# Seven-product feed-forward kernel: the planner's transfer times, SP costs and conversion dates changed

## The chip, the cores and the metric

The kernel runs on one core of a Trainium2 chip. The metric is the device time of one execution in microseconds (us), here always on that one core. Five engines work side by side, each through its own list of instructions in order: TensorE (PE, the matmuls; PEld is its weight load), VectorE (DVE), ScalarE (ACT), GpSimd (POOL, unused here after the start) and SyncE (SP), which issues nearly all DMA transfers. An engine whose next instruction waits for something executes nothing behind it meanwhile.

## What is computed

A channel attention over 6016 tokens of 256 channels feeds two feed-forward layers with 2048 hidden columns:

```python
qn = q / (norm(q, axis=1) + 1e-6);  kn = k / (norm(k, axis=1) + 1e-6)
s = kn.transpose(0, 2, 1) @ qn / tau            # 256 x 256
a = exp(s - s.max(-1));  a /= a.sum(-1) + 1e-9
x = v @ a
x = square(maximum(x @ w_in1, 0)) @ w_out1      # layer 1
out = leaky(x @ w_in2, 0.01) @ w_out2           # layer 2
```

The weights of both layers arrive as 64-bit floats and are turned into 32-bit ones on the chip.

## The kernel before

**Tiling.** The tokens are cut into six passes of two halves, each half 512 tokens wide (448 in the fifth pass): `WIDTH`, `NP` = 6. The hidden columns are cut into eight groups of 256, `NG` = 8. A unit is one group of one pass of one layer, 96 in all, numbered n. Every operand is split into a high and a low part (`round` or `cast` on ACT makes the high part, `low` on DVE the rest), and a product is three matmuls. From the second pass on, the first product of a unit is computed in seven block products instead of eight (F1 to F7, `product`), with sums of blocks of x and of weights prepared beforehand; ACT copies and DVE additions (`c11`, `c22`, `c21`, `c12`, lines 564 and 566) put the results together as c. The second products (`second`, `shared`) add into the banks y.

**Stages.** The attention takes the first 50 us. Layer 1 has a first pass, in which the weights of layer 1 are converted (`convert`) and folded with the attention (`fold`), and five more; layer 2 has six. During a pass of layer 1 the x of the next pass is prepared (`prepare_x`): two halves of v are loaded (`load_v`, line 236, each as four DMAs), DVE transposes them into the single buffer `xr` (line 245), ACT and DVE split them into the x tiles (line 1148 and `low`, line 116) and DVE forms differences (lines 1154 and 1157). The outputs of a pass of layer 1 leave the y banks at the start of the next pass (`take_out`, line 747, into a buffer o; `put` stores it in two DMAs), and layer 2 reads them back (`load` in `prepare_x`, line 1131). The weights of layer 2 are converted in sixteen units during layer 1: `u.load` (line 144) brings 512 KB into one of three buffers `wst`, DVE and ACT work on them, `u.round` writes the buffer `wis` (one only) for eleven of the sixteen, and `u.store` (lines 213 and 215) puts the result into DRAM. `load_wi` (lines 1185 and 1213) and `load_wo` (line 1227 and following) bring them back for every unit.

**The order.** Nothing is ordered by hand. `build` makes a list of tasks: engine, cost, due time, dependences, and the buffers taken and used. `link` sorts each kind of buffer by due time; a buffer's taker waits for the users of the one as many places back as there are buffers, and starts after the taker just before it in the line. `simulate` is a list scheduler: each engine that is free takes, among its tasks that are ready, the one with the earliest due time. A task that depends on another is ready `lat` after that one's end. The starts found are the order in which the instructions are emitted. Only this order reaches the chip: the engines there wait on semaphores, not on planned times. `build` runs three times, each with the starting times (`base[n]`) of the one before. The unit of time is one 512-column matmul. DVE and ACT steps cost what they take (3 for an addition of 512 columns, 5.4 for a `low` of 1024). Every SP task costs 1, however many DMAs it issues, and its data is taken as landed `LOAD` = 22 later (the read-back of x: 55).

**Due times that matter here.** With t0 the start of a pass, the v halves of the next pass are due at t0 + 46 and t0 + 76, the o buffers at t0 + 44 and t0 + 74; both are of the kind `v`, of which there are three. The transposes are due from t0 + 100 on. The conversions of layer 2 are due evenly between the start of the third pass (`base[2 * NG]`) + 60 and the start of layer 2 (`base[6 * NG]`) - 60; their weight loads are due 72 units ahead of that and become ready when the first pass has ended (`begin`) and a `wst` buffer is free.

```python
b.alloc.deps += line[k - b.bufs].users          # link
x = min((x for x in open_[e] if x.ready <= t), key=lambda x: x.due)   # simulate
```

Of the kernel before, what the change touches and what calls it, by code (L numbers as in the profile page):

```python
# [31 lines left out]
def attn_moe_moe2(  # L32
# [715 lines left out]


    tasks, lines = [], {}  # L750

    class Buf:

# [5 lines left out]
    class Task:  # L759


        def __init__(self, engine, cost, due, fn, *args, deps=(), alloc=None, uses=(), lat=0.3):
            self.engine, self.cost, self.due, self.fn, self.args = engine, cost, due, fn, args
            self.deps = [x for x in deps if x is not None]
            self.order, self.lat, self.start = [], lat, None
            self.item = None
            if alloc is not None:
                alloc.alloc = self
                alloc.users.append(self)
            for b in uses:  # L770
                b.users.append(self)
            tasks.append(self)
# [12 lines left out]
    def simulate(pe):  # L785
        for x in tasks:
            x.then, x.then_order = [], []
        for x in tasks:
            x.left, x.ready = len(x.deps) + len(x.order), 0
            for d in x.deps:  # L790
                d.then.append(x)
            for d in x.order:
                d.then_order.append(x)
        free = {"DVE": 13, "ACT": 6, "POOL": 0, "SP": 0, "PE": 0}
        open_ = {e: [] for e in free}
        for x in tasks:
            if not x.left:
                open_[x.engine].append(x)
        n = len(tasks)
        while n:  # L800
            best = None
            for e in ("DVE", "ACT", "POOL", "SP"):
                if open_[e]:
                    t = max(free[e], min(x.ready for x in open_[e]))
                    if best is None or t < best[0]:
                        best = t, e
            t = pe.when(free["PE"])
            if t is not None and (best is None or t < best[0]):
                best = t, "PE"
            if best is None:  # L810
                raise RuntimeError(["stuck"] + [(x.fn.__name__, x.args, [(d.fn.__name__, d.args) for d in x.deps + x.order if d.start is None][:3]) for x in tasks if x.start is None][:12])
            t, e = best
            if e == "PE":
                x = pe.choose(t)
            else:
                x = min((x for x in open_[e] if x.ready <= t), key=lambda x: x.due)
                open_[e].remove(x)
            x.start, x.end = t, t + x.cost
            free[e] = x.end
            n -= 1  # L820
            for d in x.then + x.then_order:
                d.left -= 1
                if x in d.order:
                    d.ready = max(d.ready, t)
                if x in d.deps:
                    d.ready = max(d.ready, x.end + (0 if d.engine == e and x.lat < 1 else x.lat))
                if not d.left and d.engine != "PE":
                    open_[d.engine].append(d)
        return free

    KEEP = 4
    LOAD = 22
    GAPS = {"F2": 1, "F3": 1, "F4": 2}

    class PE:
# [72 lines left out]
    def build(base):  # L908
# [10 lines left out]
        def T(*a, **k):  # L919
            return Task(*a, **k)  # L920
# [18 lines left out]
        def convert(u, due, loaded=None, first=None, pace=4, begin=0):  # L939
            L, g = u.L, u.g  # L940
            d = lambda i: due + i * pace
            blocks = u.blocks
            if loaded is None:
                w = Buf("wst", 3, d(-12))
                t = T("SP", 1, d(-12), u.load, alloc=w, lat=LOAD, deps=[begin] if begin else ())
                deps = [t]
            else:
                w, deps = loaded, ()
            if u is first_o:
                ce = ce_b[0]  # L950
                t = None
            else:
                ce = Buf("ce", 2, d(0))
                t = T("DVE", 1.9, d(0), u.exponent, deps=deps, alloc=ce, uses=[w])
            re = T("ACT", 2.7, d(0.5), u.rebias, deps=[t], uses=[ce])
            cm = Buf("cm", 2, d(1))
            t = T("DVE", 1.9, d(1), u.mantissa, deps=deps, alloc=cm, uses=[w])
            ml = T("DVE", 3, d(2), u.mantissa_low, deps=[t], uses=[w, cm])
            t = T("DVE", 3, d(3), u.sign, deps=[re, ml], uses=[w, ce])
            if blocks:  # L960
                raw_ = Buf("whl", 2, d(4))
                t = T("DVE", 3, d(4), u.high, deps=[t], alloc=raw_, uses=[ce, cm])
                for i in range(4):
                    t = T("DVE", 1.1, d(4.2 + i / 10), lambda i=i: (sums if u.kind == "i" else out_sums)(u.x)[i](),
                          deps=[t], uses=[raw_])
                to = Buf("wis", 1, d(5))
                t = T("ACT", 4.6, d(5), u.round, deps=[t], alloc=to, uses=[raw_])
                t = T("DVE", 5.2, d(6), u.low, deps=[t], uses=[raw_, to])
            else:
                t = T("DVE", 3, d(4), u.high, deps=[t], uses=[ce, cm])  # L970
                if (u.kind, L) == ("o", 1):
                    to = wo_b[1, 0, g] = Buf("wo", 4, d(5))
                elif u.kind == "i":
                    to = whl_b[g] = Buf("whl", 2, d(5))
                else:
                    to = Buf("whl", 2, d(5))
                t = T("ACT", 2.7, d(5), u.round, deps=[t], alloc=to, uses=[cm])
                t = T("DVE", 3, d(6), u.low, deps=[t], uses=[cm, to])
            if u.kind == "o" or L == 2:
                stores[u.kind, L, g] = T("SP", 1, d(7), u.store, deps=[t], uses=[to], lat=LOAD)  # L980
            return t

        whl_done = {0: None, 1: None}
# [15 lines left out]
        for n in range(NG):  # L999
# [3 lines left out]
            if g + 1 < NG:  # L1003
# [7 lines left out]
                lo = [T("DVE", 2.5, at0(m["fold_low"] + 2.6 * i), lambda i=i, pw=pw: fold_low(i, *pw[i]), deps=[hi[i]], uses=[b])  # L1011
                      for i in range(KC)]
                pw_after = lo
                stores["i", 1, g + 1] = T("SP", 1, at0(m["fold_low"] + 6), store_folded, g + 1, deps=lo, uses=[b], lat=LOAD)
                wi_ready[1, 0, g + 1] = lo[-1]
            wi = wi_b[1, 0, g]
            cs = [Buf("c", 3, at0(m["relu"][0 if half == 0 else 2])) for half in range(2)]
# [47 lines left out]
        def finish_plain(L, p):  # L1065
# [4 lines left out]
            for half in range(2):  # L1070
# [8 lines left out]
                else:  # L1079
                    a = T("ACT", 2.7 * s, due, take_out, key, 0, deps=done[L, p, half, 0], alloc=o)  # L1080
                b = T("DVE", 3.1 * s, due + 0.1, take_out, key, 1, deps=done[L, p, half, 1] + [a], uses=[o])
                stores["y", L, p, half] = T("SP", 1, due + 3, put, key, deps=[a, b], uses=[o], lat=LOAD)
                if (L, p) == (1, NP - 1) or p < NP - 1:
                    q = (L, p + 1) if p < NP - 1 else (2, 0)
                    for d, t in enumerate((a, b)):
# [7 lines left out]
        def prepare_x(L, p):  # L1093
# [17 lines left out]
            if L == 1:  # L1111
                vs = []
                for half in range(2):
                    v_b[p, half] = Buf("v", 3, t0 + (46, 76)[half])
                    vs.append(T("SP", 1, t0 + (46, 76)[half], load_v, p, half, alloc=v_b[p, half], lat=LOAD))
                for j, (kc, half) in enumerate(((0, 0), (1, 0), (0, 1), (1, 1))):
                    i = SLOT[kc, half]

# [9 lines left out]
            else:  # L1128
# [1 line left out]
                    new()  # L1130
                    nc.sync.dma_start(raw_x(0, 4), x2_d[p][:, :, :w])

                t = T("SP", 1, t0 + 30, load, alloc=xr, lat=2.5 * LOAD, deps=[stores["y", 1, p, 0], stores["y", 1, p, 1]])
                ready.update(dict.fromkeys(range(4), t))

            def split_x(which, i, j, after):
# [40 lines left out]
        def load_wi(n):  # L1177
            L, p, g = units[n]
            b = wi_b[n] = Buf("wi", 3, base[n - 2] + 0.5)
            if n < 2 * NG:  # L1180
# [18 lines left out]
                    nc.sync.dma_start(wi_d[L, g][:, :, 4:], raw(r["w"][:, :, 4:]))  # L1199

                e = base[n] - 12
                t = T("SP", 1, base[n - 2] + 0.5, load, alloc=b, lat=LOAD, deps=[stores.get(("i", 1, g))])
                xb = Buf("whl", 2, e - 25)
                t = T("DVE", 3, e - 25, join, deps=[t], alloc=xb, uses=[b])
                for i in range(4):
                    t = T("DVE", 1.1, e - 20 + i, lambda i=i: r["s"][i](), deps=[t], uses=[xb])
                t = T("ACT", 2.7, e - 10, high, deps=[t], uses=[xb, b])
                wi_ready[n] = T("DVE", 3, e - 5, lows, deps=[t], uses=[xb, b])
                stores["i", 1, g, "s"] = T("SP", 1, e, store, deps=[wi_ready[n]], uses=[b], lat=LOAD)
                return  # L1210

            def load():
                nc.sync.dma_start(raw(wi_tile(L, p, g)[:, :, 1:]), wi_d[L, g][:, :, 1:])

            dep = stores["i", 1, g, "s"] if L == 1 else stores["i", 2, g]
            wi_ready[n] = T("SP", 1, base[n - 2] + 0.5, load, alloc=b, lat=LOAD, deps=[dep])

        def load_wo(n):
            L, p, g = units[n]
# [2 lines left out]
            if form_of(n) == "P":  # L1222
# [3 lines left out]
                        src = src[:, :, :4].rearrange("p a (k b) m -> p a k b m", k=KC)  # L1226
                    nc.sync.dma_start(raw(wo_tile(L, p, g)), src)

                wo_ready[L, p, g] = T("SP", 1, base[n] + 13, load, alloc=b, lat=LOAD, deps=[dep])
                return  # L1230

            def load():
# [8 lines left out]
                t = late_w[n, "S23"] = cpool.tile([P, 2, 2, P], F32R, tag="ce", name="ws")  # L1241
                nc.sync.dma_start(raw(t), wo_d[L, g][:, :, 6:])

            wo_ready[L, p, g] = T("SP", 1, base[n] + 13, load, alloc=b, lat=LOAD, deps=[dep])
            b = wo_b[n, "S1"] = Buf("ws", 2, base[n] + 20)
            wo_ready[n, "S1"] = T("SP", 1, base[n] + 20, load_s1, alloc=b, lat=LOAD, deps=[dep])
            b = wo_b[n, "S23"] = Buf("ce", 2, base[n] + 60)
            wo_ready[n, "S23"] = T("SP", 1, base[n] + 60, load_s23, alloc=b, lat=LOAD, deps=[dep])


        def unit(n):
# [233 lines left out]
        def combine(p):  # L1485
# [27 lines left out]
            for half, parts in enumerate(((("X", 0, y21), ("P1", 1, y11)), (("V", 0, y22), ("U", 1, y12)))):  # L1513
# [3 lines left out]
                for i, (which, d, dep) in enumerate(parts):  # L1517
# [4 lines left out]

                    k = dict(alloc=o, uses=[B[p, which]]) if i == 0 else dict(uses=[o, B[p, which]])
                    ts_.append(T("DVE", 3.1 * s, t0 + 120 + 30 * half + 15 * i, go, deps=[dep, *ts_], **k))
                T("SP", 1, t0 + 80 + 20 * half, put, key, deps=ts_, uses=[o], lat=LOAD)

        conv = [Unit(kind, 2, g) for g in range(NG) for kind in "io"]
        for sweep in range(2 * NP):
# [65 lines left out]
```

## Time and profile before

| | us |
|---|---|
| median of 3 runs | 1058.67 (1057.12 to 1059.61) |
| the profiled execution | 1054.96 |
| its span, first to last instruction | 1053.2 |
| PE busy | 1027.8 (98%) |
| DVE busy | 766.3 (73%) |
| ACT busy | 753.9 (72%) |
| DMA queue of SP | 209.48 MB, 60.9% of 16 engines |

The profile shows one execution. Rows of a timeline give start, duration, engine, line, operation, out<-in, and in brackets how long the engine had been idle before it and what released it. The granted clock is the share of TensorE's full speed that was allowed in a stretch.

### The profile page before, as it was taken

To read this page: it belongs to the slowest core of one execution; us is meant where nothing else is said; L and a number is where in the kernel's file an instruction comes from. 1 tells how busy PE (TensorE), PEld (TensorE's weight loads), DVE (VectorE), ACT (ScalarE), POOL (GpSimd) and SP (SyncE) were. 2 spreads that over 40 slices of the span, in tenths; PEclk is the share of its full clock that TensorE was granted. 3 is DMA by queue.
4 is the path that set the end of the run, shared out by engine and by line. 5 is a ranking of instruction groups with operands and counts; after the bars stand their busy time and mean duration, and the time that the engine had idled before them with its cause. 6 is when DMAs were issued, how large, how long until landed. Compare 5 with 4: busy or idle time off the path is not lost.

```text
span 1053.2 us, 12842 instructions
## 1 busy us (share of the span) xinstructions
PE 1027.8 (98%) x4723; PEld 868.1 (82%) x4723; DVE 766.3 (73%) x1082; ACT 753.9 (72%) x1140; POOL 0.7 (0%) x6
## 2 busy tenths in 40 slices
PE   9999999998989999799999999999999999999997
PEld 8888887886878788698888888888888888998886
DVE  5999889997888964556546777877877887776433
ACT  6798877886787776468767777677677677675653
POOL 0000000000000000000000000000000000000000
PEclk9999999999999999899999999999999999999999
DMA  9785497589779575556535455555655654644521
GB/s 349 261 220 180 159 288 255 174 313 305 223 275 316 198 248 169 146 191 221 168 125 196 169 185 209 174 181 194 177 188 191 184 184 165 192 180 168 177 76 40
DMA packets 118623, 210.96 MB, mean 200 GB/s; under 512 B 49056, under 2 KB 60320, under 8 KB 116512
## 3 DMA queue, kind: packets, MB, share of 16 engines
q1 hardware_dynamic: 117840, 209.48, 60.9%
q8 instruction: 37, 0.61, 0.3%
q10 hardware_dynamic: 720, 0.66, 0.2%
q14 instruction: 26, 0.21, 0.1%
HBM read 171.05 MB, written 39.06 MB: 199 GB/s over the span
## 4 chain that ended last, share of the span: by engine, by line
PE 87%; DMA 7%; DVE 2%; SPq 1%; ACT 1%; issue 0%; ACTq 0%; DVEq 0%
PE y L557 38%; PE ha L557 16%; PE hb L557 12%; PE hc L557 5%; PE h L713 4%; DMA v<-in_v_dram 4%; PE he L557 4%; PE yA L557 3%; PE sT L399 2%; PE y L597 2%; SPq L236 1%; PE pw L265 1%; DMA qk<-in_k_dram 1%; DMA wi<-wis 1%; PE yF L557 1%; DVE xr L245 1%
## 5 line engine op out<-in xcount | busy, mean ns | idle before, releaser
L557 PE MATMUL y<-g,wo 128*128 128x512 f32 (+1 forms) x1938 | 495.9, 386 | 0.0
L557 PEld LDWEIGHTS y<-g,wo 128*128 128x128 f32 x1938 | 365.5, 189 | 68.4
L116 DVE TENSOR_TENSOR g<-c,g 128x1024 fp32r<-128x1024 f32 (+1 forms) x192 | 229.4, 1199 | 44.5 <-ACT g L683 37.5
L557 PE MATMUL ha<-x,wi 128*128 128x512 f32 (+1 forms) x768 | 214.4, 388 | 16.7 <-ACT w L1270 11.9
L557 PEld LDWEIGHTS ha<-x,wi 128*128 128x128 f32 x768 | 143.9, 189 | 45.4 <-ACT w L1270 13.1
L683 ACT CAST g<-c 128x1024 fp32r<-128x1024 f32 (+1 forms) x162 | 167.4, 1034 | 4.1
L557 PE MATMUL hb<-x,wi 128*128 128x512 f32 (+1 forms) x576 | 160.7, 387 | 0.3 <-DVE c L564 0.3
L557 PEld LDWEIGHTS hb<-x,wi 128*128 128x128 f32 x576 | 108.9, 189 | 21.0 <-DVE c L564 0.7
L700 ACT ACTIVATE c<-c 128x512 f32<-128x512 f32 (+1 forms) x144 | 89.7, 623 | 41.5 <-DVE c L566 41.4
L698 ACT ACTIVATE c<-c 128x512 f32<-128x512 f32 (+1 forms) x160 | 97.6, 619 | 27.0 <-DVE c L564 25.6
L557 PE MATMUL hc<-x,wi 128*128 128x512 f32 (+1 forms) x288 | 80.0, 386 | 0.0
L1270 ACT COPY w<-ha 128x512 f32<-128x512 f32 (+1 forms) x64 | 37.0, 578 | 59.5 <-PE ha L557 59.4
L566 DVE TENSOR_TENSOR c<-w,hb 128x512 f32<-128x512 f32 (+1 forms) x44 | 29.7, 674 | 50.5 <-ACT w L1270 50.0
L557 PEld LDWEIGHTS hc<-x,wi 128*128 128x128 f32 x288 | 53.8, 188 | 10.2 <-ACT c L1270 0.4
L557 PE MATMUL he<-x,wi 128*128 128x512 f32 (+1 forms) x216 | 60.2, 387 | 1.0 <-DVE c L564 1.0
L566 DVE TENSOR_TENSOR c<-u,hb 128x512 f32<-128x512 f32 (+1 forms) x44 | 29.7, 674 | 35.5 <-PE hb L557 35.4
L1148 ACT CAST x<-xr 128x1024 fp32r<-128x1024 f32 (+3 forms) x44 | 40.2, 926 | 17.3 <-DVE xr L245 17.1
L1270 ACT COPY u<-ha 128x512 f32<-128x512 f32 (+1 forms) x64 | 36.7, 573 | 21.1 <-PE ha L557 21.1
L116 DVE TENSOR_TENSOR x<-xr,x 128x1024 fp32r<-128x1024 f32 (+3 forms) x44 | 46.6, 1065 | 3.2 <-ACT x L1148 3.2
L557 PEld LDWEIGHTS he<-x,wi 128*128 128x128 f32 x216 | 40.2, 188 | 9.4 <-DVE c L564 1.8
L713 PE MATMUL h<-x,wi 128*128 128x512 f32 x192 | 47.9, 391 | 0.0
L1270 ACT COPY c<-ha 128x512 f32<-128x512 f32 (+1 forms) x64 | 36.6, 572 | 12.4 <-PE ha L557 10.8
(130 smaller groups left out, 1082.1 us busy)
## 6 DMA issues: line engine op xcount, KB each, us to landing
wi<-wi SPq DMA_DIRECT2D x80, 896.0 KB, 5.8
wo<-wo SPq DMA_DIRECT2D x96, 512.0 KB, 4.1
wi<-wi SPq DMA_DIRECT2D x24, 512.0 KB, 4.6
wst<-in_moe_w_in_dram SPq DMA_DIRECT2D x16, 512.0 KB, 5.6
wst<-in_moe_w_out_dram SPq DMA_DIRECT2D x16, 512.0 KB, 5.5
wi<-wis SPq DMA_DIRECT2D x8, 1024.0 KB, 6.4
x<-o SPq DMA_DIRECT2D x20, 256.0 KB, 5.1
xr<-x SPq DMA_DIRECT2D x5, 1024.0 KB, 4.8
```

The costliest lines, as they stand in the source:

```text
L116: tt(lo, x, raw(hi), op=ALU.subtract)
L236: nc.sync.dma_start(v_t[p, half][b * B : (b + 1) * B, :n], src)
L399: nc.tensor.matmul(sT[j][:, :C], t[:, 0, i, j * P : (j + 1) * P], t[:, 1, i], start=n == 0 and i == 0, stop=last_tile and i == g - 1,)
L557: nc.tensor.matmul(ps, a[m], b[n], start=first and i == 0, stop=i == 2, skip_group_check=True)
L566: tt(to, a, b, op=ALU.add)
L597: nc.tensor.matmul(y_bank(L, p, 1, t // 2)[:, t % 2 * C : (t % 2 + 1) * C], gt[:, a, fb, t * P : (t + 1) * P], wo[:, b, :, fb], start=(g, ...
L683: nc.scalar.copy(g_t[n, half][:, 0, :, :w], c)
L698: nc.scalar.activation(c, c, AF.Square)
L700: nc.scalar.activation(c, c, AF.Prelu, alpha=0.01)
L713: nc.tensor.matmul(h_t[n, half, fb][:, :w], a[i], b[j], start=start, stop=stop, skip_group_check=True)
L1148: nc.scalar.copy(part(0), src())
L1270: nc.scalar.copy(to, h(0))
```

## The change

Only the planner's numbers change; no instruction is added or removed.

1. An SP task has a kind, and the kind sets its cost on SP (`COST`) and the time until it lands (`LAT`): for v 10 and 50 instead of 1 and 22, and so on.
2. The v halves are due at t0 + 30 and t0 + 60 (`VDUE`).
3. A task may have a `release`, before which it isn't ready. The weight loads of the conversions for layer 2 get their due time less 60.

```diff
+    COST = {"v": 10, "out": 9, "y": 5, "wi": 2.6, "wo": 1.6, "wst": 2, "store": 2, "x": 1.6}
+    LAT = {"v": 50, "wi": 34, "wo": 26, "wst": 36, "store": 34, "x": 55}
...
-        def __init__(self, engine, cost, due, fn, *args, deps=(), alloc=None, uses=(), lat=0.3):
+        def __init__(self, engine, cost, due, fn, *args, deps=(), alloc=None, uses=(), lat=0.3, release=0):
+            if engine == "SP":
+                cost, lat = COST.get(cost, 2.3), LAT.get(cost, 30)
...
-            self.order, self.lat, self.start = [], lat, None
+            self.order, self.lat, self.start, self.release = [], lat, None, release
...
-            x.left, x.ready = len(x.deps) + len(x.order), 0
+            x.left, x.ready = len(x.deps) + len(x.order), x.release
...
+    VDUE = 30, 60
...
-                t = T("SP", 1, d(-12), u.load, alloc=w, lat=LOAD, deps=[begin] if begin else ())
+                t = T("SP", "wst", d(-12), u.load, alloc=w, lat=LOAD, deps=[begin] if begin else (),
+                      release=d(-12) - 60 if begin else 0)
...
-                stores[u.kind, L, g] = T("SP", 1, d(7), u.store, deps=[t], uses=[to], lat=LOAD)
+                stores[u.kind, L, g] = T("SP", "store", d(7), u.store, deps=[t], uses=[to], lat=LOAD)
...
-                stores["y", L, p, half] = T("SP", 1, due + 3, put, key, deps=[a, b], uses=[o], lat=LOAD)
+                stores["y", L, p, half] = T("SP", "out" if L == 2 else "y", due + 3, put, key, deps=[a, b], uses=[o], lat=LOAD)
...
-                    v_b[p, half] = Buf("v", 3, t0 + (46, 76)[half])
-                    vs.append(T("SP", 1, t0 + (46, 76)[half], load_v, p, half, alloc=v_b[p, half], lat=LOAD))
+                    v_b[p, half] = Buf("v", 3, t0 + VDUE[half])
+                    vs.append(T("SP", "v", t0 + VDUE[half], load_v, p, half, alloc=v_b[p, half], lat=LOAD))
...
-                t = T("SP", 1, t0 + 30, load, alloc=xr, lat=2.5 * LOAD, deps=[stores["y", 1, p, 0], stores["y", 1, p, 1]])
+                t = T("SP", "x", t0 + 30, load, alloc=xr, lat=2.5 * LOAD, deps=[stores["y", 1, p, 0], stores["y", 1, p, 1]])
...
-                t = T("SP", 1, base[n - 2] + 0.5, load, alloc=b, lat=LOAD, deps=[stores.get(("i", 1, g))])
+                t = T("SP", "wi", base[n - 2] + 0.5, load, alloc=b, lat=LOAD, deps=[stores.get(("i", 1, g))])
...
-            wo_ready[L, p, g] = T("SP", 1, base[n] + 13, load, alloc=b, lat=LOAD, deps=[dep])
+            wo_ready[L, p, g] = T("SP", "wo", base[n] + 13, load, alloc=b, lat=LOAD, deps=[dep])
...
-                T("SP", 1, t0 + 80 + 20 * half, put, key, deps=ts_, uses=[o], lat=LOAD)
+                T("SP", "out", t0 + 80 + 20 * half, put, key, deps=ts_, uses=[o], lat=LOAD)
```

The remaining loads and stores (of folded weights, of sums, the other loads of wi and wo) are renamed in the same way.

## Rows read from the trace of the kernel before

**Rows 1.** Page, part 1: busy us (share of the span), instructions.

```profile
PE 1027.8 (98%) x4723; PEld 868.1 (82%) x4723; DVE 766.3 (73%) x1082; ACT 753.9 (72%) x1140; POOL 0.7 (0%) x6
```

**Rows 2.** Stretches: busy us (instructions) of PE, PEld, DVE, ACT, POOL; clock, DMA.

```profile
70.00:130.00 60.00, 60.00 (x294) 50.70 (x293) 53.77 (x89) 50.06 (x74) 0.00 (x0) 1.00 0.52 171
...
200.00:300.00 100.00, 92.38 (x399) 75.43 (x398) 84.15 (x138) 74.05 (x112) 0.00 (x0) 0.98 0.82 269
300.00:400.00 100.00, 97.43 (x421) 79.55 (x420) 77.20 (x118) 75.75 (x115) 0.00 (x0) 0.98 0.73 246
400.00:500.00 100.00, 93.07 (x439) 83.60 (x438) 56.69 (x70) 67.61 (x108) 0.00 (x0) 0.97 0.60 190
500.00:600.00 100.00, 100.00 (x443) 82.90 (x442) 58.48 (x69) 71.89 (x107) 0.00 (x0) 1.00 0.50 170
...
700.00:800.00 100.00, 100.00 (x442) 82.75 (x442) 77.43 (x101) 72.75 (x113) 0.00 (x0) 1.00 0.56 183
```

**Rows 3.** Waits of PE, whole span: total us, times, longest us.

```profile
PE ha L557 <- ACT w L1270: 11.9, 3, 6.9
PE ha L557 <- ACT c L1270: 4.8, 2, 3.0
...
PE he L557 <- DVE c L564: 1.0, 2, 0.8
```

**Rows 4.** Timeline from 234 to 257 us.

```profile
234.40 3.90 SPq L236 DMA_DIRECT2D v<-in_v_dram  x4
...
245.35 0.71 DVE L245 STREAM_TRANSPOSE xr<-v 128x512 f32<-128x512 f32 x1 [3.24 <-DMA v<-in_v_dram]
...
248.91 0.96 PE L557 MATMUL ha<-x,wi 128*128 128x512 f32 x3 [1.82 <-ACT c L1270]
...
253.89 1.30 DVE L245 STREAM_TRANSPOSE xr<-v 128x512 f32<-128x512 f32 x2 [3.20 <-DMA v<-in_v_dram]
...
256.81 0.96 PE L557 MATMUL ha<-x,wi 128*128 128x512 f32 x3 [2.83 <-ACT w L1270]
```

**Rows 5.** Timeline from 342 to 346 us.

```profile
342.06 0.65 DVE L245 STREAM_TRANSPOSE xr<-v 128x448 f32<-128x448 f32 x1 [2.93 <-DMA v<-in_v_dram]
...
345.88 0.98 PE L557 MATMUL ha<-x,wi 128*128 128x512 f32 x3 [2.14 <-ACT w L1270]
```

**Rows 6.** Timeline from 421 to 436 us.

```profile
421.10 4.37 SPq L236 DMA_DIRECT2D v<-in_v_dram  x4
...
432.52 1.30 DVE L245 STREAM_TRANSPOSE xr<-v 128x512 f32<-128x512 f32 x2 [7.93 <-DMA v<-in_v_dram]
...
435.39 1.49 PE L557 MATMUL ha<-x,wi 128*128 128x448 f32 x3 [6.93 <-ACT w L1270]
```

**Rows 7.** Timeline from 280 to 297 us.

```profile
280.20 0.55 SPq L215 DMA_DIRECT2D wi<-wis  x1
...
290.38 1.05 ACT L205 CAST wis<-wr 128x1024 fp32r<-128x1024 f32 x1 [4.08 <-DMA wi<-wis]
...
296.80 1.65 PE L557 MATMUL ha<-x,wi 128*128 128x512 f32 x3 [2.96 <-ACT c L1270]
```

**Rows 8.** Stretches of 5 us that hold a restart of PE.

```profile
295.00:300.00 5.00, 3.20 (x8) 2.58 (x9) 4.75 (x10) 3.23 (x6) 0.00 (x0) 0.66 0.65 216
...
345.00:350.00 5.00, 3.86 (x11) 2.85 (x12) 4.76 (x7) 4.45 (x7) 0.00 (x0) 0.74 0.20 79
...
435.00:440.00 5.00, 4.61 (x13) 4.14 (x14) 3.90 (x7) 3.89 (x7) 0.00 (x0) 0.54 0.00 0
```

**Rows 9.** Line 144's output-weight loads: duration ns min/median/max, first and last start us.

```profile
L144 SPq DMA_DIRECT2D wst<-in_moe_w_out_dram x16: 367/384/1208, 34.8 to 331.0; - x16
```

**Rows 10.** Timeline: outputs leaving the banks, and the last use of xr.

```profile
241.42 0.69 DVE L747 COPY o<-y 128x512 f32<-128x512 f32 x1
...
264.84 1.23 DVE L116 TENSOR_TENSOR x<-xr,x 128x1024 fp32r<-128x1024 f32 x1 [0.35 <-ACT x L1148]
...
576.11 0.57 ACT L747 COPY o<-y 128x512 f32<-128x512 f32 x1
```

More of the change, by code (lines that the diff above doesn't have):

```diff
@@ L1013, in build @@
                 pw_after = lo
-                stores["i", 1, g + 1] = T("SP", 1, at0(m["fold_low"] + 6), store_folded, g + 1, deps=lo, uses=[b], lat=LOAD)
+                stores["i", 1, g + 1] = T("SP", "store", at0(m["fold_low"] + 6), store_folded, g + 1, deps=lo, uses=[b], lat=LOAD)
                 wi_ready[1, 0, g + 1] = lo[-1]
@@ L1208, in load_wi @@
                 wi_ready[n] = T("DVE", 3, e - 5, lows, deps=[t], uses=[xb, b])
-                stores["i", 1, g, "s"] = T("SP", 1, e, store, deps=[wi_ready[n]], uses=[b], lat=LOAD)
+                stores["i", 1, g, "s"] = T("SP", "store", e, store, deps=[wi_ready[n]], uses=[b], lat=LOAD)
                 return
@@ L1215, in load_wi @@
             dep = stores["i", 1, g, "s"] if L == 1 else stores["i", 2, g]
-            wi_ready[n] = T("SP", 1, base[n - 2] + 0.5, load, alloc=b, lat=LOAD, deps=[dep])
+            wi_ready[n] = T("SP", "wi", base[n - 2] + 0.5, load, alloc=b, lat=LOAD, deps=[dep])
         def load_wo(n):
@@ L1242, in load_s23 @@
                 nc.sync.dma_start(raw(t), wo_d[L, g][:, :, 6:])
-            wo_ready[L, p, g] = T("SP", 1, base[n] + 13, load, alloc=b, lat=LOAD, deps=[dep])
+            wo_ready[L, p, g] = T("SP", "wo", base[n] + 13, load, alloc=b, lat=LOAD, deps=[dep])
             b = wo_b[n, "S1"] = Buf("ws", 2, base[n] + 20)
-            wo_ready[n, "S1"] = T("SP", 1, base[n] + 20, load_s1, alloc=b, lat=LOAD, deps=[dep])
+            wo_ready[n, "S1"] = T("SP", "wo", base[n] + 20, load_s1, alloc=b, lat=LOAD, deps=[dep])
             b = wo_b[n, "S23"] = Buf("ce", 2, base[n] + 60)
-            wo_ready[n, "S23"] = T("SP", 1, base[n] + 60, load_s23, alloc=b, lat=LOAD, deps=[dep])
+            wo_ready[n, "S23"] = T("SP", "wo", base[n] + 60, load_s23, alloc=b, lat=LOAD, deps=[dep])
         def unit(n):
```

## The prediction

> **What bounds the kernel now.** I read the engines' busy time first, then the span cut into stretches, then what TensorE (PE) waited for, then the order of time around each wait. PE is busy 1027.8 of 1053.2 us [rows 1], so the matmuls themselves are the floor and only the rest can move. The stretches show where that rest lies. From 70 to 130 us, and from 500 us until near the end, PE has no gap; between 200 and 500 us it is busy 92.38, 97.43 and 93.07 of each 100 us [rows 2]. Its list of waits adds up to the same: 11.9 + 4.8 + 1.0 = 17.7 us in eight waits [rows 3]. By name the releaser is a ScalarE (ACT) or VectorE (DVE) step of the product chain, an instruction of half a microsecond, so the name isn't the cause; one step further back is needed.
>
> The order of time gives it, at the start of each of the first layer's later passes. The SP queue starts the four parts of a v load at 234.40 us; DVE, which works strictly in order, has a transpose of that v next and sits 3.24 us until 245.35; its second sits 3.20 us until 253.89. Behind each stands a DVE addition that empties a bank, and PE idles 1.82 and 2.83 us [rows 4]. The same pair appears near 342 us (2.93 of DVE, 2.14 of PE) [rows 5] and near 432 us, where DVE waits 7.93 us and PE 6.93 us [rows 6]. These transposes are not urgent: they prepare x for a pass that begins some 80 us later. They hurt only because the plan put them in DVE's queue at a moment when it believed the transfer done. One wait is of another kind: the store of the buffer wis, issued at 280.20, holds ACT 4.08 us until 290.38, and PE idles 2.96 us at 296.80 [rows 7].
>
> Each long wait costs a second time. In the 5 us that hold the restart the granted clock is 0.66, 0.74 and 0.54, so part of each is at 1.2 instead of 2.4 GHz [rows 8].
>
> **The change, part by part.** One unit of the planner is one 512-column matmul; from 500 to 600 us 443 of them fill 100.00 us [rows 2], so a unit is 0.226 us.
>
> *Longer transfers, SP charged per issue.* The old plan gives every load 1 unit on SP and lets it land 22 later, 23 units or 5.2 us, after its issue begins. In the trace the first v load took 245.35 - 234.40 = 10.9 us [rows 4], the last 432.52 - 421.10 = 11.4 us [rows 6]. The new plan gives v 10 + 50 = 60 units, 13.6 us: above both. The transposes then stand behind work that DVE can do at once. This removes the v waits: 11.9 us and, of the 4.8, 1.82 [rows 3, 4], together 13.7 us. The remaining 1.0 us [rows 3] are one wait of 0.8 behind a wi load and one of 0.2 behind a v load; wi is now given 2.6 + 34 units = 8.3 us instead of 5.2, so I count the 1.0 as gone. Nothing is added to any engine's work; the same instructions are put in another order.
>
> The Trainium skill, page "DMA: Bandwidth & Descriptors", section "Anatomy of one DMA", speaks against this part: it fits a transfer with 2.0 us plus its bytes over 436 GB/s (for the gpsimd path). By that, 512 KB of v would be an estimated 3.2 us, the old 5.2 us would already be too long, and the edit would bring nothing. The 10.9 us here speaks for the edit, and the measurement decides.
>
> *Earlier v.* VDUE moves the halves from 46 and 76 units after a pass begins to 30 and 60. The shift itself is 16 units, 3.6 us. The order of the three buffers they share with the outputs o matters more. Before, a pass took them in the order o0, v0, o1, v1, so v0 could not go until the o0 of the pass just begun was started: hence 234.40. Now it is v0, o0, v1, o1: v0 waits only for buffers of the pass before and can be issued most of a pass earlier; only v1 stays behind o0. So I expect one load instead of two at a pass's start.
>
> *Even conversion.* Every load of a second-layer weight gets a release 60 units before its due time; before, it went as soon as one of three buffers was free. In the trace the last of these loads starts at 331.0 us [rows 9]. Its release lies far later. The outputs of a pass are due 74 units (second half) and 44 units (first half) into the next one; they leave at 241.42 and 576.11 us [rows 10], so the third pass starts near 225 and the second layer near 566 us. The sixteen conversions are spread over the 327 us between, less 60 units: one every 20.4 us, the last load's release near 515. So the conversion now runs until about 520 us. Its DVE work follows from the stretches: 84.15 and 77.20 us of DVE per 100 us with it, 56.69 and 58.48 after it [rows 2], so about 25 us per 100. Spread over some 300 us this gives 400 to 500 us about 82 and takes from 200 to 300. It costs nothing as long as DVE keeps up, and 700 to 800 us shows DVE at 77.43 with PE at 100.00, 70 to 130 us DVE at 53.77 of 60 with PE at 60.00 [rows 2]. If this cover fails, a mishap costs about what the wis wait did, 2.96 us [rows 7]; a gain beyond the waits counted here is excluded, since PE has no other gap there. Two conversions now stand some 20 us apart; the wis store took 10.1 us (280.20 to 290.38), so the round waits for no store any more: 2.96 us saved.
>
> *Clock.* After the wis wait 8 matmuls take 3.20 us where 1.8 would do; near 345 us 11 take 3.86 instead of 2.5; after 435 us 13 of 448 columns take 4.61 instead of 2.6 [rows 8]. That is 1.4 + 1.4 + 2.0 = 4.8 us, which go with the waits.
>
> *The first pass and the second layer.* The first pass gets new orders too, with DVE at 90% of 70 to 130 us [rows 2]. Its fold loads were due 48 units ahead of the conversion that reads them and now are planned to land after 2 + 36, so I charge nothing; the bounds are zero and one wait like those above, 2 to 3 us. The second layer (500 us on) has no gap to win; costs of 9 for an output store shift orders by a few units, between zero and the same 2 to 3 us.
>
> **Sum.** 13.7 + 1.0 + 2.96 + 4.8 = 22.5 us at most. Against it I set 2.5 us, about one wait of the middle size [rows 5, 7], for whatever the new orders bring. Net 20.0 us. The profiled execution took 1054.96 us: 1054.96 - 20.0 = 1035. The median of the runs is 3.7 us above it; transfers that land later in those runs may be part of that, but one trace can't tell, so I leave the 3.7 in: 1038.7 us.
>
> **The rivals.**
> *The second half of v is still late.* v1 stays behind o0 on the same queue, and the new allowance of 13.6 us exceeds the worst landing by only 2.2 us; if SP is that much behind its plan, DVE stands again. Then the three waits after second halves, 2.83 + 2.14 + 6.93 = 11.9 us [rows 4 to 6], and the clock of two of them (3.4 us) remain: 22.5 - 11.9 - 3.4 = 7.2 us gain, 1051.5. For it: the worst wait followed a second half. Against: transfers are less crowded without the eager conversion and with one v load at a time.
>
> *Nothing changes.* The waits move to another load that DVE reads in order, or v lands later by as much as is allowed. For it: DMA landing times are not constant. Against: 13.6 against 11.4 us. Time: 1057 to 1060.
>
> *Slower, by the shared buffers.* In the new order o1 takes over the buffer of v0, three places back, so the output of a pass's second half can't leave PSUM until v0 has been transposed. Near 241 us it left at 241.42 [rows 10], the transpose came at 245.35 and its twin a microsecond later [rows 4]. If v0 stayed where it is, the copy would slip by about 6 us and PE's second products with it, at four pass starts: 24 us lost against 17.7 won, with the low clock kept: about 1065. It decides if v0 isn't transposed before the pass starts. Against: v0's load can start early, and the single buffer xr that the transposes write is free from 264.84 + 1.23 us on [rows 10] until the next pass's transposes, so the plan has some 70 us of room for them.
>
> **How the numbers follow.** Forecast (waits gone, 1032 to 1044) 0.60; second half late (1044 to 1055) 0.20; nothing (within 0.2%, 1056.5 to 1060.8, about what a measurement can tell from no change) 0.08; slower 0.12. Likeliest: 1038.7 us. Range: the low end is all 22.5 us from the median, and 4 us less because the run may also lose the 3.7: 1032; the high end takes in most of the second case: 1054. That leaves about 0.2 out. Faster 0.80, same 0.08, slower 0.12.
>
> **What would show it.** Right: DVE's waits for v fall from the 3 to 8 us of [rows 4 to 6] to under 1 each; PE's idle time from 200 to 500 us under 3 us with a clock of 1.00; first-half v loads issued tens of microseconds before the pass start; the last weight load for the conversion near 515 us; DVE at about 80 per 100 us from 200 to 500. Wrong: a take-out of o waiting for a transpose of v; DVE waits on v of the old size; new gaps of PE before 130 or after 500 us.

## The result, and the profile after

The changed kernel takes 1030.91 us (median of 4 runs, 1030.72 to 1031.22) against 1058.7 us: a ratio of 0.974, 95% interval 0.972 to 0.976, a gain of 27.8 us. The forecast was 1038.7 with a range from 1032 to 1054; the direction and the mechanism were right, the gain was larger than the whole sum of 22.5 us, and the time lies 1.1 us below the range.

The profiled execution took 1031.22 us, its span 1029.4 us. First the page's parts 1 and 2 of the changed kernel, then its stretches, columns as in [rows 2]:

```profile
PE 1021.3 (99%) x4723; PEld 863.9 (84%) x4723; DVE 768.2 (75%) x1082; ACT 753.8 (73%) x1140; POOL 0.7 (0%) x6
...
PEclk9999999999999999999999999999999999999999
```

```profile
70.00:130.00 60.00, 60.00 (x294) 50.71 (x293) 54.47 (x90) 49.85 (x73) 0.00 (x0) 1.00 0.55 181
200.00:300.00 100.00, 100.00 (x442) 82.20 (x441) 75.24 (x113) 76.67 (x116) 0.00 (x0) 1.00 0.74 235
300.00:400.00 100.00, 100.00 (x445) 83.14 (x444) 75.74 (x112) 77.12 (x118) 0.00 (x0) 1.00 0.74 246
400.00:500.00 100.00, 100.00 (x476) 88.96 (x475) 80.56 (x119) 79.68 (x126) 0.00 (x0) 1.00 0.80 271
```

The counts of the engines' instructions are those of [rows 1]. PE, which had 92.38, 97.43 and 93.07 in these hundreds [rows 2], now has 100.00 in each, at a granted clock of 1.00. DVE is spread evenly at 75 to 81. PE's list of waits, which answers [rows 3], holds only the start of the kernel:

```profile
PE warm L364 <- DVE small L358: 1.1, 1, 1.1
PE sT L399 <- DMA qk<-in_k_dram: 0.7, 1, 0.7
PE eT L492 <- ACT e L486: 0.3, 1, 0.3
```

The place of [rows 4] in the changed kernel, from its timeline (the first two lines are the first half of the v of the fourth pass, the next two its second half, the last is the load of the fifth pass's first half):

```profile
161.50 2.13 SPq L236 DMA_DIRECT2D v<-in_v_dram  x4
...
197.41 0.71 DVE L245 STREAM_TRANSPOSE xr<-v 128x512 f32<-128x512 f32 x1
...
231.49 3.08 SPq L236 DMA_DIRECT2D v<-in_v_dram  x4
...
246.85 1.30 DVE L245 STREAM_TRANSPOSE xr<-v 128x512 f32<-128x512 f32 x2
...
248.18 1.90 SPq L236 DMA_DIRECT2D v<-in_v_dram  x4
```

The first half is loaded at 161.50 us instead of 234.40, and the transposes of the second stand 15.4 us behind its issue; neither transpose carries a wait. The transfers themselves are little faster: one part of a v load (a load is four) landed in 2.9 to 9.7 us, median 5.1, against 2.7 to 9.0, median 6.0, before. The last weight load of the conversion starts at 490.2 us instead of 331.0 [rows 9]:

```profile
L144 SPq DMA_DIRECT2D wst<-in_moe_w_out_dram x16: 367/510/1167, 35.2 to 490.2; - x16
```

The gain can be read from two numbers of the profile. PE's busy time fell by 6.5 us (1027.8 to 1021.3): the same matmuls, fewer of them at 1.2 GHz (0.3 of it lies in the first 50 us, at a clock of 1.00 in both). The rest of the span, in which PE was idle, fell from 25.4 to 8.1 us, by 17.3. Together 23.8 us of span. The remaining 4 us of the medians' difference are the subject of two runs below.

### The profile page after: what moved, and what is told of

It is laid out like the page before. It is cut to its first block, busy times and chain, and to the rows that moved or that the text cites. A ratio compares the mean times of both kernels' runs of the same rounds, so it can differ in the third digit from the quotient of the medians.

```text
span 1029.4 us, 12821 instructions
## 1 busy us (share of the span) xinstructions
PE 1021.3 (99%) x4723; PEld 863.9 (84%) x4723; DVE 768.2 (75%) x1082; ACT 753.8 (73%) x1140; POOL 0.7 (0%) x6
## 4 chain that ended last, share of the span: by engine, by line
PE 98%; DMA 1%; ACT 0%; DVE 0%; issue 0%; SPq 0%
PE y L557 43%; PE ha L557 17%; PE hb L557 12%; PE hc L557 6%; PE he L557 5%; PE h L713 4%; PE sT L399 3%; PE yA L557 3%; PE y L597 2%; PE pw L265 1%; PE yF L557 1%; DMA qk<-in_k_dram 1%; ACT e L486 0%; PE pn L373 0%; ACT whl L205 0%; DVE cm L178 0%
## 5 line engine op out<-in xcount | busy, mean ns | idle before, releaser
L399 PE MATMUL sT<-qk 128*128 128x256 f32 x188 | 42.0, 384 | 0.7 <-DMA qk<-in_k_dram 0.7
```

Source lines behind the costliest of these rows:

```text
L399: nc.tensor.matmul(sT[j][:, :C], t[:, 0, i, j * P : (j + 1) * P], t[:, 1, i], start=n == 0 and i == 0, stop=last_tile and i == g - 1,)
```

## The experiments

The theory: DVE stands before v because the plan takes transfers as landed too early. Rivals: the eager conversion crowds the transfers (B); the order of the shared buffers decides (C). Each run's time is compared with the kernel before on the same chip, whose medians were 1058.76, 1057.75 and 1058.2 us for the three groups of four.

**The three parts alone.** Costs and landing times alone (the edit is shown against the changed kernel):

```diff
-    VDUE = 30, 60
+    VDUE = 46, 76
...
-                      release=d(-12) - 60 if begin else 0)
+                      release=0)
```

> The new SP costs and landing times alone; v dates and conversion loads as before. Theory A (DVE stood because the plan took transfers as landed too early): DVE's waits for v, 19.0 us before, fall under 2; only the wait behind the store of wis may stay, as its new 8.2 us are below the 10.1 us it took: 1031 to 1036 us. Rival B (the eager conversion crowds the transfers and delays v): waits for v of 3 us and more remain, 1050 to 1056 us. Rival C (the dates of v decide, through the order of the shared buffers): at least the waits after second halves remain, 1045 to 1055 us.

1031.69 us (1030.73 to 1032.98), ratio 0.975 (0.973 to 0.976). Nearly the whole gain. PE keeps one wait of 0.2 us after the start. DVE's waits for v are 1.5 us in one wait; for wis ACT waits 1.8 us in two. Neither B nor C is needed for it: the conversion was as eager as before (DVE at 92.57 of the 100 us from 200 on) and both halves of v were loaded at a pass's start.

The release alone (against the kernel before):

```diff
+                      release=d(-12) - 60 if begin else 0)
```

> The release of the conversion's weight loads alone; costs, landing times and v dates as before. Theory A: the wait behind the store of wis goes (2.96 us of PE and 1.4 us of low clock), the waits for v stay near 14 us of PE: 1050 to 1055 us. Rival B: v lands earlier without the crowd and DVE's waits for v fall under 5 us: 1033 to 1042 us.

1051.42 us (1044.89 to 1054.36), ratio 0.992 (0.989 to 0.995): as theory A has it, but with a cost that neither side expected. DVE's waits for transfers, from the list of waits of this run:

```profile
DVE xr L245 <- DMA v<-in_v_dram: 15.2, 4, 5.0
DVE ce L149 <- DMA wst<-in_moe_w_in_dram: 12.6, 5, 4.0
DVE ce L149 <- DMA wst<-in_moe_w_out_dram: 5.0, 2, 3.2
```

The wait on wis is gone, the one on v smaller by a fifth, and 17.6 us of waits on the conversion's own weight loads have come, where there were 0.5. Loaded eagerly, these lay ready before DVE came to them; released late, they meet the same 5.2 us of the plan, and from 225 us on they took 5.1 to 10.7 us to land, median 7.4.

The v dates alone (against the kernel before):

```diff
-                    v_b[p, half] = Buf("v", 3, t0 + (46, 76)[half])
-                    vs.append(T("SP", 1, t0 + (46, 76)[half], load_v, p, half, alloc=v_b[p, half], lat=LOAD))
+                    v_b[p, half] = Buf("v", 3, t0 + (30, 60)[half])
+                    vs.append(T("SP", 1, t0 + (30, 60)[half], load_v, p, half, alloc=v_b[p, half], lat=LOAD))
```

> The v dates 30 and 60 alone. Theory A: first halves land a pass earlier and their waits go (1.8 us of PE), those after second halves stay (11.9 us of PE) with their low clock: 1053 to 1058 us. Rival C: most of DVE's 19.0 us of waits for v go: 1035 to 1045 us.

1041.27 us (1038.61 to 1042.52), ratio 0.984 (0.982 to 0.986). What theory A gave missed; the time lies in rival C's range. So the dates are a second cure for the same waits, enough for 17.5 us without any new allowance. DVE's waits for v fell from 19.0 us to 3.9 in two. The timeline at the places of [rows 4] and [rows 6] shows which loads are left:

```profile
237.97 4.48 SPq L236 DMA_DIRECT2D v<-in_v_dram  x4
...
249.09 0.72 DVE L245 STREAM_TRANSPOSE xr<-v 128x512 f32<-128x512 f32 x1 [3.36 <-DMA v<-in_v_dram]
...
251.02 1.97 SPq L236 DMA_DIRECT2D v<-in_v_dram  x4
...
263.73 1.22 DVE L116 TENSOR_TENSOR x<-xr,x 128x1024 fp32r<-128x1024 f32 x1
264.98 1.17 DVE L245 STREAM_TRANSPOSE xr<-v 128x448 f32<-128x448 f32 x2
...
404.31 2.35 SPq L236 DMA_DIRECT2D v<-in_v_dram  x4
...
412.62 0.71 DVE L245 STREAM_TRANSPOSE xr<-v 128x512 f32<-128x512 f32 x1 [0.51 <-DMA v<-in_v_dram]
```

Both waits are of a second half, and they are what the first half waited at the same places before: 3.36 us against 3.24, 0.51 against 0.45 (and none against 1.24 between them). The loads that remain go about when the first ones went. What is gone is the three waits of the loads that went second (3.20, 2.93 and 7.93 us). After the last of them (404.31) no second load goes. At the others two still go one behind the other, 237.97 and 251.02 as 234.40 and 247.28 before. But the second is now the first half of the next pass, and its transposes write `xr`, which this pass uses until 264.95: they come 14.0 us behind the issue, where the second load had 6.6 before. The dates thus lengthen the same distance, from issue to use, by another way. PE's waits that are left, 7.6 us, stand mostly behind other transfers: 3.1 behind loads of wi, 2.6 behind the store of wis, 1.9 behind v.

**Which transfer.** Only v's allowance changed in the kernel before (10 and 50 instead of 1 and 22; the SP tasks carry their kinds as in the changed kernel), and then its complement:

```diff
-        def __init__(self, engine, cost, due, fn, *args, deps=(), alloc=None, uses=(), lat=0.3):
+        def __init__(self, engine, cost, due, fn, *args, deps=(), alloc=None, uses=(), lat=0.3, release=0):
+            if engine == "SP":
+                cost, lat = (10, 50) if cost == "v" else (1, 2.5 * LOAD if cost == "x" else LOAD)
```

> The kernel before with one pair of numbers changed: a v load costs 10 on SP and lands 50 later; all else as before. Theory: v is what DVE stood for, so its waits for v fall under 2 us and PE keeps only the wait behind the store of wis (3.0 us and 1.4 us of low clock) and the 0.8 us behind wi: 1033 to 1039 us. Rival (the allowances of all transfers are needed, since the plan's times of all queues hang together): 1042 to 1052 us.

1035.81 us (1034.29 to 1037.15), ratio 0.980 (0.977 to 0.983). DVE waits for v no more. What is left is the other kind, as forecast, one conversion further on (timeline):

```profile
283.17 0.42 SPq L213 DMA_DIRECT2D wo<-wis  x1
...
292.73 1.04 ACT L205 CAST wis<-wr 128x1024 fp32r<-128x1024 f32 x1 [3.73 <-DMA wo<-wis]
...
294.32 0.97 PE L557 MATMUL ha<-x,wi 128*128 128x512 f32 x3 [3.07 <-ACT w L1276]
```

All other times new, v at its old 1 and 22 (these lines against the changed kernel; the v dates and the release as in the kernel before):

```diff
-    COST = {"v": 10, "out": 9, "y": 5, "wi": 2.6, "wo": 1.6, "wst": 2, "store": 2, "x": 1.6}
-    LAT = {"v": 50, "wi": 34, "wo": 26, "wst": 36, "store": 34, "x": 55}
+    COST = {"v": 1, "out": 9, "y": 5, "wi": 2.6, "wo": 1.6, "wst": 2, "store": 2, "x": 1.6}
+    LAT = {"v": 22, "wi": 34, "wo": 26, "wst": 36, "store": 34, "x": 55}
```

> The complement: all new SP costs and landing times except those of v, which stay at 1 and 22; v dates and conversion loads as before. Theory: DVE's waits for v stay at 12 to 20 us: 1050 to 1056 us, and the runs spread over more than 3 us. Rival: under 1045 us.

1045.11 us (1043.55 to 1046.01), ratio 0.989 (0.985 to 0.993). The expectation missed: it gains 12.6 us, where 1050 to 1056 us would have been 2 to 8. DVE's waits for v are 15.2 us as expected, but the longest fell:

```profile
413.38 4.97 SPq L236 DMA_DIRECT2D v<-in_v_dram  x4
...
424.96 1.30 DVE L245 STREAM_TRANSPOSE xr<-v 128x512 f32<-128x512 f32 x2 [4.37 <-DMA v<-in_v_dram]
```

The load takes as long as in [rows 6], 11.6 us against 11.4, yet DVE stands 4.37 us instead of 7.93: it reached the transpose later. PE's waits after the start are 10.6 us instead of 18.0. Why the other times put more of DVE's work ahead of this transpose, the runs don't show. The gains of the two halves (21.9 and 12.6 us) add up to more than the whole, so they overlap.

An allowance between the two, 1 and 34, in the kernel before:

```diff
+                cost, lat = (1, 34) if cost == "v" else (1, 2.5 * LOAD if cost == "x" else LOAD)
```

> The kernel before with v at 1 on SP and 34 until landed, 7.9 us in all, between the old 5.2 and the new 13.6; all else as before. Theory (each load costs what it lands later than planned): the loads that took 6.6 to 8.6 us wait no more, those of about 11 us wait about 3: DVE's waits for v 4 to 10 us, 1039 to 1050 us. Rival (any allowance that puts DVE's own work first will do): as with 13.6 us, 1034 to 1037 us.

1042.77 us (1041.69 to 1045.15), ratio 0.985 (0.982 to 0.987), waits for v as follows:

```profile
DVE xr L245 <- DMA v<-in_v_dram: 6.9, 3, 3.7
```

So 5.2, 7.9 and 13.6 us of allowance give 19.0, 6.9 and no us of waits, and medians of about 1058, 1043 and 1036 us, in the order that the theory asks for. Load by load it doesn't hold:

```profile
247.32 2.84 SPq L236 DMA_DIRECT2D v<-in_v_dram  x4
...
254.75 1.30 DVE L245 STREAM_TRANSPOSE xr<-v 128x512 f32<-128x512 f32 x2 [3.71 <-DMA v<-in_v_dram]
```

This load needed 7.4 us from its first issue, less than the 7.9 allowed, and DVE still stood 3.71 us. SP had itself stood 2.0 us just before it, by its list of waits behind the store of an output; an issue that comes later than planned then uses up the allowance as a late landing does. Of PE's 8.3 us of waits in this run 4.2 stand behind v, 3.4 behind the store of wis. With the costs and landing times alone, too, the one wait for v that was left, 1.5 us, ended 10.4 us after the first issue, with 13.6 allowed.

**One part left out of the whole.** These edits are against the changed kernel. With v back at 1 and 22 (the same two lines as above):

> The changed kernel with v back at 1 and 22; new v dates, release and all other times stay. Theory: the second halves of v, loaded at a pass's start, are transposed 5.2 us after their issue in the plan, so DVE waits up to three times by 2 to 5 us: 1035 to 1042 us, runs spread over 2 us or more. Rival (with the v dates and the even conversion the allowance of v no longer matters): 1030 to 1033 us, spread under 1 us.

1035.47 us (1034.96 to 1037.51), ratio 0.980 (0.977 to 0.983): three waits for v, 6.5 us together, and 4.7 us for weight loads. As the theory had it. But v's allowance is not the only way to most of the gain: without it the rest of the change still gains 22.3 us, as much as the allowance alone (21.9).

With all costs and landing times back:

```diff
-                cost, lat = COST.get(cost, 2.3), LAT.get(cost, 30)
+                cost, lat = 1, 2.5 * LOAD if cost == "x" else LOAD
```

> The changed kernel with all SP costs and landing times back at 1 and 22; v dates 30 and 60 and the release stay. Theory: the first halves of v are safe, the second halves are not, and with the release the weight loads of the conversion are a new kind that DVE meets before they land, as in the run with the release alone (17.6 us of DVE's waits on them): 1038 to 1048 us. Rival (the two together suffice): 1031 to 1035 us.

1046.62 us (1044.09 to 1046.74), ratio 0.990 (0.987 to 0.993): 9.6 us of waits for v, 14.5 for weight loads. Dates and release together do worse than the dates alone.

Without the release, and without the v dates (each by its line above):

> The changed kernel without the release: the conversion runs early again; new times and v dates stay. Theory: with the allowances right, DVE waits little whether it is busy or not; the store of wis takes longer than its 8.2 us once or twice and DVE at 90% from 200 to 300 us has no room: 1030.5 to 1033 us. Rival (the even conversion carries a part of its own): 1034 us or more.

1031.83 us (1031.36 to 1032.56), ratio 0.974 (0.972 to 0.976). The waits behind the store of wis that the expectation allowed for did not come.

```profile
200.00:300.00 100.00, 100.00 (x443) 82.80 (x442) 92.60 (x153) 84.48 (x127) 0.00 (x0) 1.00 0.89 292
```

> The changed kernel with the v dates 46 and 76; new times and release stay. Theory: both halves are loaded at a pass's start, but the plan gives them 13.6 us: DVE's waits for v stay under 2 us, 1030.5 to 1032.5 us. Rival (the early first half is needed): waits for v of 3 us or more, 1034 us or more.

1032.3 us (1031.53 to 1035.48), ratio 0.976 (0.972 to 0.979). Once the allowances are right each brings about a microsecond, which these intervals don't tell from nothing; with both gone the first run above still gave 1031.69. The row of the run without the release shows that an early conversion is no burden: DVE at 92.60 and PE at 100.00.

**How much the kernel before varies.** The same kernel, profiled twice more:

> The kernel before, unchanged, profiled a second time. Theory: the runs of before differ by up to 4.6 us because DVE's waits end with transfers that land at other times in each run; PE's waits between 130 and 500 us (17.9 us in the first profile) then differ between the two profiles by about as much as their times do (within 0.5 us). Rival: the difference lies elsewhere (start, end, or spread over the span), and PE's waits there agree within 0.5 us.

1055.19 us under the profiler, 0.23 above the first profile; PE's waits were 17.0 us instead of 18.0, less in the longer profile, so the expectation failed on both sides; the two times are too near each other to tell more. The runs without a profile went up to 1062.93.

> The kernel before, unchanged, a third profile. Two profiles gave 1054.96 and 1055.19 us, the median without a profile is 1058.8. Theory (the waits differ from execution to execution, and the two were low by chance): the third lies anywhere from 1054 to 1063, and as likely above 1057 as not. Rival (an execution under the profiler is regularly shorter for this kernel): 1054.5 to 1055.7 again.

1057.77 us, so an execution under the profiler is not regularly as short as the first two, though all three lie below the medians without a profile. Its page:

```profile
span 1056.0 us, 12842 instructions
...
PE 1029.5 (97%) x4723; PEld 868.6 (82%) x4723; DVE 766.0 (73%) x1082; ACT 753.6 (71%) x1140; POOL 0.7 (0%) x6
```

It is 2.8 us longer than the first, 1.7 of it in PE's busy time (more matmuls at the low clock) and 1.1 in idle time; DVE's waits for v are 21.7 us instead of 19.0. In the second profile they were 21.1 us at nearly the first one's time, so they don't set the time by themselves.

**What the runs leave open.** All ten edits of the plan gained, also the two that left v's numbers alone (all but v, and the release). An order changed at random, with every allowance and date as before, was not run, so a part of each single gain may come from the new order as such. SP cost and landing time of v were not changed apart. What the profiles share is that the span goes with PE's waits after the start: 18.0 us (before), 16.8 (release alone), 10.6 (all but v), 8.3 (7.9 us allowed), 7.6 (dates alone), 3.4 (v alone) and none (the whole), with spans of 1053.2, 1052.6, 1042.5, 1041.6, 1038.5, 1032.5 and 1029.4 us.

## Why the prediction was right or wrong

- **What bounds the kernel, and the v waits: right.** The waits that [rows 4 to 6] name as DVE standing before a transfer are gone, and the run with v's allowance alone shows that the allowance is enough for it; the dates are another way. I counted 13.7 + 0.2 us of idle time and 3.4 of clock for it, 17.3; alone it gave 21.9 against its own group's median. One reading was wrong and cost nothing: the 17.7 us of [rows 3] are seven waits, an eighth of 0.3 us makes 18.0.
- **Longer transfers, 13.6 against 11.4 us: right.** In the changed kernel the new allowance held for every v load. The fit of the Trainium skill (page "DMA: Bandwidth & Descriptors", section "Anatomy of one DMA — SWDGE (gpsimd) path"), by which 512 KB would land in an estimated 3.2 us, is stated for the gpsimd path; for these loads, which SP issues, it falls short. In the kernel before, DVE had to wait for loads 6.6 to 11.4 us after their first issue.
- **Earlier v: the order of the buffers right, its worth and the rival built on it wrong.** I gave the dates no term of their own in the sum; alone they bring 17.5 us. As forecast, the first half goes most of a pass ahead. But two loads still stand near a pass's start (231.49 and 248.18), the second being the next pass's first half. My first rival said the *second halves'* waits would stay. In the run with the dates alone a second half waits only what the first half waited at that place, 3.36 and 0.51 us, and the waits of the load behind it are gone, since `xr` puts its use off.
- **The shared buffers as a way to be slower: it did not decide.** The transposes of the first half are done by 198.82 + 0.70 us, and the output that takes that buffer leaves at 237.71 us.
- **Even conversion: the size of its own part was wrong.** I gave it the 2.96 us of wis and 1.4 of clock. The new costs and landing times alone, the store's among them, remove all but 0.2 us of PE's waits, and the run without the release is only 0.9 us above the whole change. Its dates were right: the last load was put near 515 us with the pass starts of before, and it starts at 490.2 with these some 24 us earlier.
- **Clock: the term of the sum that was mis-sized, and the step that took the time below the range.** 4.8 us in the sum, 6.5 measured as PE's busy time. I worked the loss out from the count of matmuls in three stretches of 5 us. The next stretch after the second one was still low:

```profile
350.00:355.00 5.00, 5.00 (x21) 4.05 (x21) 3.46 (x7) 3.38 (x7) 0.00 (x0) 0.92 0.51 184
```

  Read from the clock column instead (the missing share of 5 us), an estimate, the three stretches of [rows 8] give 1.7, 1.3 and 2.3 us and this one 0.4, 5.7 together. Another 0.3 us lies in the first 50 us. Where the last half microsecond lies the rows don't show.
- **The 2.5 us set aside for new waits: not needed.** The changed kernel has none after the start, nor in the second layer.
- **The 3.7 us between the profile and the median: the step that failed in the forecast itself.** I carried them over as if they belonged to the runs. The changed kernel's four runs lie within 0.5 us, and its median 0.3 us below its profile; the four runs of the kernel before beside them spread over 2.5 us (1051.9 to 1065.3 over the runs on all chips). The third profile shows its excess in idle time and the clock; that the runs without a profile are longer for the same reason is argued from that and from the spread, not shown, since they have no trace.

The miss of 7.8 us adds up: 2.5 set aside, 3.7 carried over, 0.3 by which the profiled execution of the changed kernel lies above its median, 1.3 of span beyond the sum (PE's busy time 1.7 more, idle time 0.4 less than counted). The low end of the range, 1032, had already taken the 2.5 and the 3.7 in; what lies below it is the clock term and the 0.3.

## What to carry to other kernels

Where an order is planned ahead and each engine works strictly in order, the time allowed for a transfer must cover the worst landing in the trace, counted from the start of its first issue, and the time by which that issue comes late; with 7.9 us instead of 13.6 the median was 7 us higher here (on another chip), and allowances above 13.6 us were not tried. Putting the use of a transfer off, by dates or by a buffer, does the same. Moving loads later, or spreading them, is only safe once that allowance is right: the release alone brought 17.6 us of new waits. Take the gain from the medians, not only from one profile: here the medians give 27.8 us and the two profiles 23.7. The whole change's runs spread less than those before, 0.5 us against 2.5; not every run without waits for v did (4.0 us without the new dates).

## What the runs showed of the hardware

SP's issue of the four DMAs of a v load took from 1.90 us (changed kernel, at 248.18) to 5.72 us (costs and landing times alone, at 313.83):

```profile
313.83 5.72 SPq L236 DMA_DIRECT2D v<-in_v_dram  x4
```

The Trainium skill, page "DMA: Bandwidth & Descriptors", section "Issuing engines are not separate DMA queues", calls the sequencer's time for an issue usually small beside the transfer. For the long ones of these it isn't: in the run with all times but v's, 4.97 of the 11.6 us from first issue to transpose were issue. An SP cost of 10 units, 2.3 us, lies inside that spread, so for the long ones it is the landing time of 50 units that has to cover the rest; the two were not changed apart.
